# Overlapping feature tiles, B turned on its way from DRAM, and one packed state unit for two chunks, in a fused S5 scan and gated MLP

## The chip, the cores and the metric

The kernel runs on one core of a Trainium2 chip. The time is device time in microseconds from start to end of one execution; a lower number is better. In the profile PE is the matmul engine (PEld its weight loads), DVE the vector engine, ACT the scalar engine, POOL the general engine, and SP the engine that here only issues DMAs. Every engine works through its own list of instructions in order.

## The reference

Tokens x (2048 rows of 448 features, bf16) are normalised per row. The normalised rows xn go two ways, and the results are joined:

```python
xn = _layernorm(x)
# A: diagonal complex recurrence with 448 states
Bu = einsum("bld,pd->blp", xn + 0j, ((Lam_bar - 1.0) / Lam)[:, None] * Bmat)
h_t = Lam_bar * h_(t-1) + Bu_t
s = 2.0 * einsum("blp,dp->bld", hseq, Cmat).real + xn * Dskip
# B: gated MLP with 1792 inner features
h = sigmoid(xn @ w_gate) * (xn @ w_up)
g = silu(h @ w_down)
out = x + s * g
```

## The kernel before

The 2048 tokens are worked in four chunks of 512, which this document numbers 0 to 3 as the code does. A product over features needs features on partitions, so each chunk's xn is turned into `xnT[c]`, four tiles of 128 rows by 512 tokens (chunk 3 uses the buffer of chunk 0). Since 448 is three and a half times 128, the fourth tile holds the last 64 features twice, once in each half of the partitions: the columns 384 to 447 of xn are copied behind column 447 (`ln_turn`, `ln_twice`) before the turn. Chunk 0 is turned on PE, the other chunks by DMA turns on SP (L270).

**Work in half rows.** From the fifth feature group on, every product contracts 64 partitions at a time. PE runs a matmul on partitions 0-63 beside one on partitions 64-127 (`beside_each`); such a pair is called a slot here. A `Unit` is a list of products for the top half and one for the bottom half. `gu_unit(c, ft)` makes gate and up projection of one group of 128 inner features: 7 products in each half, two PSUM banks. `bu_unit(c, pt)` makes the inputs of the states: pt 0 to 2 hold 128 states each, real and imaginary part in a bank each, 7 and 7 products. The last 64 states (pt 3) hold real and imaginary part in the two halves of one bank, with 4 products on top and 3 below. `duo` runs two units: first the top of a beside the bottom of b, then the top of b beside the bottom of a. Both halves of a sum go to the same bank; when a sum changes halves, `Sum.add` sends a word over POOL so that the first half has ended.

**Order.** `emit_line` writes the order by hand. A positive number is a group of inner features, a negative one a state unit (-4 is pt 3). Chunks 1 to 3 run

```python
(0, -1), (1, -2), emit_downs, (2, 3), (4, -3), (5, 6), (-4, 7), (8, 9), (10, 11), (12, 13)
```

with `emit_downs` the down projection of the chunk before, and `emit_ys` the output product of the chunk before, behind (12,13) in chunk 1 and ahead of it in chunks 2 and 3. The eight PSUM banks are handed out in turn (`bank`). After a duo ACT empties its banks (`empty`: sigmoid or copy), and DVE multiplies (L737). The scan and its rotations (`bu_after`) are cut into pieces with a cost each; `fill` gives them out in the room that PE's slots leave, first come first served. `at` and `rest` hang other steps on a group: the normalisation of the next chunk, the turns, the mixing of C.

**B and C.** B is loaded into `raw["b_re"]` and `raw["b_im"]`, the last 64 columns are doubled, and SP turns it into `bT` by eight DMA turns (`emit_b`, L297), a pair per pt. C comes later into two raw buffers: c_re in the place called `raw_c`, c_im in `raw_re` (the place of b_re). It is turned behind groups 0 and 1 of chunk 1 (`emit_c_turn`, L169) and mixed with the state scales by `emit_c`: ACT writes a scaled copy (L482) into a temporary tile, DVE adds the other part (L483). The first three mixings hang on the second quarter of chunk 1's `emit_downs`. `c_room` gives the temporaries: the first two lie in `raw_im`, the place of b_im, the next two and the last in a pool, the fifth and sixth in `raw_c`.

**SP's order around this.** First x, weights for groups 0-3, B, weights for 4-7, x of chunk 1. Then the first two turns of B around the last weights (`load_w`, four DMAs a call: gate, up, and the last 64 rows of each, L122 and L126), the skip vector, the other turns, x of chunk 2, the turns of chunk 1's xn in two pairs with the last turns of B between them, `wd` (L1025), C (L165), and the swap of halves for unit -4 (L530).

Of the kernel before, what the change touches and what calls it, by code (L numbers as in the profile page):

```python
# [29 lines left out]
NPK = 2 * D  # L30
EPS = 1e-5
# [7 lines left out]
def swap_pair(ap: bass.AP) -> bass.AP:  # L39
    step_p, n_p = ap.ap[0]  # L40
    step_m, n_m = ap.ap[1]
    step_f, n_f = ap.ap[2]
    assert n_m == 2
    return bass.AP(tensor=ap.tensor, offset=ap.offset + step_m,
                   ap=[[step_p, n_p], [-step_m, n_m], [step_f, n_f]])

# [17 lines left out]
def kernel(  # L64
# [51 lines left out]
    def load_rows(eng, t, mat, f0, f1):  # L116
        eng.dma_start(out=t[:, 0:3, f0:f1], in_=mat[0:384, f0:f1].rearrange("(kt p) f -> p kt f", p=P))
        eng.dma_start(out=t[0:64, 3, f0:f1], in_=mat[384:448, f0:f1])

    def load_w(eng, f0, f1, between=None):  # L120
        for t, mat in ((wg, B_w_gate), (wu, B_w_up)):
            eng.dma_start(out=t[:, :, f0:f1], in_=mat[0:384, f0:f1].rearrange("(kt p) f -> p kt f", p=P))  # L122
        if between:
            between()
        for mat, p0 in ((B_w_gate, 0), (B_w_up, 64)):
            eng.dma_start(out=wt[p0:p0 + 64, f0:f1], in_=mat[384:448, f0:f1])  # L126
# [23 lines left out]
    for nm, mat in (("b_re", A_B_re), ("b_im", A_B_im)):  # L150
        raw[nm] = w.tile([P, KT, DP], BF16, name=nm, tag="raw" + nm[1:])
        load_rows(sync, raw[nm], mat, 0, D)
    dve.memset(raw["b_re"][:, :, D:DP], 0.0)
# [103 lines left out]
    def ln_norm(c, j):  # L257
        t = c * TPC + j
        xb = xn[c % 3]
        if c < 2:  # L260
            dve.tensor_scalar(out=xb[:, j, 0:D], in0=x_t[c][:, j, :], scalar1=mv[:, t, 0:1],
                              scalar2=rsd[:, t, :], op0=ALU.subtract, op1=ALU.mult)
        else:
            act.activation(xb[:, j, 0:D], x_t[c][:, j, :], ACT.Identity, bias=nmr[:, t, :],
                           scale=rsd[:, t, :])

    def ln_turn(c, j):
        xb, cols = xn[c % 3], slice(j * P, (j + 1) * P)
        if c > 0:
            sync.dma_start_transpose(out=xnT[c][:, 0:KT, cols], in_=xb[:, j, :])  # L270
            return
        (dve if j < 2 else pool).tensor_copy(out=xb[:, j, D:DP], in_=xb[:, j, 384:D])
        for kt in range(KT):
            pe.transpose(tps[j % 2][:, kt, :], xb[:, j, kt * P:(kt + 1) * P], ident[:])  # L274

    def ln_twice(c, copy, j0=0, j1=TPC):
        copy(out=xn[c % 3][:, j0:j1, D:DP], in_=xn[c % 3][:, j0:j1, 384:D])
        for j in range(j0, j1):
            ln_turn(c, j)
# [6 lines left out]
    def emit_b_twice():  # L286
        t = raw["b_im"]
        act.copy(out=t[:, 0:3, D:DP], in_=t[:, 0:3, 384:D])
        act.copy(out=t[0:64, 3, D:DP], in_=t[0:64, 3, 384:D])

    def emit_b(cc, pt):
        n = P if pt < 3 else 64
        if cc == 0:
            p0 = pt * P
        else:
            p0 = D if pt == 3 else 512 + pt * P
        sync.dma_start_transpose(out=bT[:, :, p0:p0 + n], in_=raw[("b_re", "b_im")[cc]][0:n, pt, :])  # L297
# [109 lines left out]
    def emit_skip(c):  # L407

        t = xn[c % 3][:, :, 0:D]
        dve.tensor_tensor(out=t, in0=t, in1=bcast_mid(skip[:], TPC), op=ALU.mult)  # L410
# [46 lines left out]
    def emit_c(i):  # L457
# [9 lines left out]
        if not c_room:  # L467
            for nm in ("raw_im", "raw_c"):
                both = []
                c_room.extend((nm, both, k) for k in range(2))  # L470
                if nm == "raw_im":
                    c_room.extend((None, None, None) for _ in range(2))
            c_room.append((None, None, None))
# [55 lines left out]
    def swap_halves(o, i):  # L529
        sync.dma_start(out=o[0:64, :], in_=i[64:128, :])  # L530
        sync.dma_start(out=o[64:128, :], in_=i[0:64, :])

    def bu_unit(c, pt):
        u = Unit()
        psts = [bank("bu") for _ in range(2 if pt < 3 else 1)]
        sums = [Sum(t, 7) for t in psts]

        def ops(h, cc, n):
            lo, hi = bu_cols(pt, cc)
            return [(sums[cc], (bT[HALF[h], kt, lo:hi], xnT[c][HALF[h], kt, :], 0, TC))  # L540
                    for kt in range(n)]

        if pt < 3:
            u.top = ops(0, 0, 4) + ops(0, 1, 3)
            u.bot = ops(1, 0, 3) + ops(1, 1, 4)
        else:
            u.top, u.bot = ops(0, 0, 4), ops(1, 0, 3)
        u.empty, u.then = bu_after(c, pt, psts)
        return u

    def bu_after(c, pt, pst):
# [5 lines left out]

        def then():
            unread[0] += 1
            assert unread[0] <= 4  # L560
            stream[0] += 1
            popped[stream[0]] = clock[0]
            pieces.extend((*p, stream[0]) for p in line)
# [62 lines left out]
        else:  # L626
            bus = sp.tile([P, TC], BF16, name="bus3", tag="bus", bufs=4)
            bsw = sp.tile([P, TC], BF16, name="bsw3", bufs=1)

            def empty_3():  # L630
                act.copy(out=bus[:], in_=pst[0][:])
                swap_halves(bsw, bus)

            empty = [empty_3]

            def q0():
                T["ta"] = sp.tile([P, TC], BF16, name="ta3", tag="ta")
                dve.tensor_tensor(out=T["ta"][:], in0=bus[:], in1=cosT[:, 3, :], op=mul)

            def q1():  # L640
                T["tb"] = sp.tile([P, TC], BF16, name="tb3", tag="tb")
                dve.tensor_tensor(out=T["tb"][:], in0=bsw[:], in1=spm[:, 3, 0, :], op=mul)
                unread[0] -= 1
# [26 lines left out]
            def q7():  # L670
                h = ht.tile([P, TC], BF16, name="h3")
# [3 lines left out]
            for cost, f, wait in ((0.42, q0, 1), (0.42, q1, 2), (0.42, q2, 0), (1.27, q3, 0), (0.42, q4, 0),  # L675
                                  (0.42, q5, 3), (0.34, q6, 0), (0.42, q7, 0)):
                later(cost, f, wait)
        return empty, then
# [13 lines left out]
    def gu_halves(c, ft, gt, ut, first, n0=0, n1=TC):  # L692
        f0, f1 = ft * P, (ft + 1) * P
        for t, p0 in ((gt, 0), (ut, 64)):
            pe.matmul(t[:, n0:n1], lhsT=wt[p0:p0 + 64, f0:f1],  # L695
                      rhs=xnT[c][p0:p0 + 64, 3, n0:n1], start=first, stop=not first)

    def gu_wholes(c, ft, gt, ut, first, n0=0, n1=TC, which=(0, 1)):
        f0, f1 = ft * P, (ft + 1) * P
        for t, wm in [((gt, wg), (ut, wu))[i] for i in which]:  # L700
            for kt in range(3):
                pe.matmul(t[:, n0:n1], lhsT=wm[:, kt, f0:f1], rhs=xnT[c][:, kt, n0:n1],  # L702
                          start=(first and kt == 0), stop=(not first and kt == 2))
# [14 lines left out]
    def gu_unit(c, ft):  # L718
# [6 lines left out]
        def ops(h, i, tail):  # L725
            x = xnT[c]
            o = [(sums[i], ((wg, wu)[i][HALF[h], kt, f], x[HALF[h], kt, :], 0, TC)) for kt in range(3)]
            return o + [(sums[i], (wt[HALF[h], f], x[HALF[h], 3, :], 0, TC))] * tail
# [61 lines left out]
    def y_ops(c, j, rows, d0=0, d1=D, skipped=False):  # L790
        sl = slice(j * P, (j + 1) * P)
        o = [(ident[rows, :], xn[c % 3][rows, j, d0:d1], d0, d1)] if skipped else []
# [21 lines left out]
    def emit_two(c, j):  # L814

        xb, two = xn[c % 3][:, j:TPC:2, 0:D], slice(j, TPC, 2)
        o = op_.tile([P, 2, D], BF16, name="o_t")
        for i in range(2):
            dve.tensor_tensor(out=o[:, i, :], in0=ys[c, j + 2 * i][:], in1=xb[:, i, :], op=ALU.add)  # L819
# [8 lines left out]
    def emit_rest_of(c, j):  # L828
        t = op_.tile([P, D], BF16, name="t_g", tag="zb", bufs=4)
        dve.tensor_tensor(out=t[:], in0=xn[c % 3][:, j, 0:D], in1=gs[c][:, j, :], op=ALU.mult)  # L830
        if j % 2 == 0:
            room_of_rests.append(w.tile([P, 2, D], FP32, name="t_x", tag=("raw_re", "raw_im")[j // 2]))
# [62 lines left out]
    def ln_plan(c):  # L895
# [16 lines left out]
        at(own, "down0", 0.0, lambda: ln_twice(c, act.copy))  # L912
# [62 lines left out]
    for pt in (0, 1, 3):  # L975
# [4 lines left out]
        if pt == 0:  # L980
            emit_b_twice()
# [25 lines left out]
    emit_b(0, 0)  # L1007
    load_w(sync, 1024, F, lambda: emit_b(1, 0))
    sync.dma_start(out=skip[:], in_=A_Dskip.partition_broadcast(P))
    for pt in range(1, KT - 1):  # L1010
        for cc in range(2):
            emit_b(cc, pt)
# [3 lines left out]
    def second_chunk(j0):  # L1016
# [3 lines left out]
        ln_twice(1, dve.tensor_copy, j0, j0 + 2)  # L1020

    at(0, 7, 1.0, lambda: second_chunk(0))
    at(0, 7, 0.0, lambda: [emit_b(cc, KT - 1) for cc in range(2)])
# [26 lines left out]
    def duo(c, a, b):  # L1050


        top, bot = a.top + b.top, b.bot + a.bot
        n = len(a.top)
        for u, t0, t1 in ((a, 0, n), (b, n, len(top))):
            beside_each(top[t0:t1], bot[t0:t1])
            if u is b:
                for i in range(2):
                    for v in (a, b):
                        if i < len(v.empty):  # L1060
                            v.empty[i]()
# [6 lines left out]
            if u is b:  # L1068
                a.then()
                b.then()  # L1070


    def emit_line(c, line):
        for p in line:
            if callable(p):
                p(c - 1)
            else:
                duo(c, *[bu_unit(c, -1 - k) if k < 0 else gu_unit(c, k) for k in p])

    emit_line(0, ((4, 5), (6, 7), (-1, 8), (-2, 9), (-3, 10), (11, 12), (-4, 13)))  # L1080
    for c in range(1, NCH):
        ends = ((12, 13), emit_ys) if c == 1 else (emit_ys, (12, 13))
        emit_line(c, ((0, -1), (1, -2), emit_downs, (2, 3), (4, -3), (5, 6), (-4, 7), (8, 9), (10, 11), *ends))
# [66 lines left out]
```

## Time and profile before

| what | value |
|---|---|
| median of three runs | 184.19 us (184.07 to 184.24) |
| span of the profiled execution | 182.6 us, granted clock 1.000 |
| the profiled execution's own time | not given beside its span; the median lies 1.6 us above the span |
| PE busy | 177.7 us, 1644 matmuls |
| DVE busy | 165.0 us |
| ACT busy | 114.1 us |
| POOL busy | 24.5 us |
| bytes moved by DMA | 15.07 MB |

A line of the timeline gives start, duration, engine, line of the kernel, operation, output and input, shape and count, and in brackets how long the engine stood before it and for whom. A line of the waits names who waited for whom, the sum in us, how many times, and the longest. A matmul's duration runs to the modelled end of its way through the array, so the distance between starts, and not the duration, tells the pace of PE. SP's lines are the times in which it issues a transfer, not the transfer itself.

### The profile page before, as it was taken

How to read it: one execution, taken by the hardware profiler on the slowest of the kernel's cores; microseconds unless marked ns; L12 is line 12 of the kernel's file. 1: busy time of each engine (PE TensorE's matmuls, PEld its weight loads, DVE VectorE, ACT ScalarE, POOL GpSimd, SP SyncE). 2: the span in 40 equal slices, each digit the busy share in tenths (PEclk: the TensorE clock that was granted, in tenths of full speed). 3: DMA queues.
4: the chain of work that ended last, by engine and by line, in shares of the span. 5: the costliest groups of instructions: out<-in, count | busy, mean ns of one | idle time of the engine just before them, and what ended most of it. 6: DMA issues, size and time to landing. Idle time of an engine off the chain costs nothing.

```text
span 182.6 us, 4348 instructions
## 1 busy us (share of the span) xinstructions
PE 177.7 (97%) x1644; PEld 98.3 (54%) x1644; DVE 165.0 (90%) x337; ACT 114.1 (63%) x236; POOL 24.5 (13%) x61
## 2 busy tenths in 40 slices
PE   7999999999999999999999999999999999999992
PEld 7776644446654444645654445545665544645552
DVE  4899999799989979999999999599999999699983
ACT  3999577979487787997367766057048567144100
POOL 4768546321000000004000000000000000000000
PEclk9999999999999999999999999999999999999999
DMA  5999997895434113011251010030001000011112
GB/s 152 312 307 252 231 161 106 229 311 111 104 76 89 29 32 101 4 52 52 41 79 29 4 29 0 4 101 0 4 2 29 4 13 17 4 50 50 29 36 68
DMA packets 27659, 15.07 MB, mean 83 GB/s; under 512 B 16243, under 2 KB 27638, under 8 KB 27638
## 3 DMA queue, kind: packets, MB, share of 16 engines
q1 hardware_dynamic: 27632, 14.79, 35.1%
q8 instruction: 13, 0.21, 0.5%
q14 instruction: 8, 0.07, 0.2%
q10 hardware_dynamic: 6, 0.00, 0.0%
HBM read 8.49 MB, written 1.84 MB: 57 GB/s over the span
## 4 chain that ended last, share of the span: by engine, by line
PE 97%; DVE 1%; POOL 0%; issue 0%; POOLq 0%; DVEq 0%
PE g_ps L510 25%; PE u_ps L510 19%; PE d_ps L510 17%; PE bu L510 12%; PE y_ps L510 11%; PE d_ps L1093 6%; PE warm_ps L192 2%; PE g_ps L702 2%; PE u_ps L702 1%; PE tp_x L274 1%; PE g_ps L695 1%; DVE sg L846 0%; DVE o_l L852 0%; DVE xnT L282 0%; POOL ident L129 0%
## 5 line engine op out<-in xcount | busy, mean ns | idle before, releaser
L510 PE MATMUL u_ps<-xnT,wu 64*128 64x512 bf16 x312 | 68.9, 376 | 0.0
L510 PE MATMUL g_ps<-xnT,wg 64*128 64x512 bf16 x312 | 62.0, 376 | 0.0
L740 ACT ACTIVATE sig<-g_ps 128x512 bf16<-128x512 f32 x52 | 29.1, 597 | 29.1 <-PE g_ps L510 29.1
L510 PE MATMUL bu<-xnT,bT 64*128 64x512 bf16 x196 | 45.7, 376 | 0.0
L510 PEld LDWEIGHTS <-wu 64*128 64x128 bf16 x312 | 25.3, 94 | 17.8 <-POOLq L512 1.6
L510 PE MATMUL d_ps<-wd,hF 64*128 64x448 bf16 x336 | 32.9, 349 | 0.0
L510 PEld LDWEIGHTS <-wg 64*128 64x128 bf16 x312 | 22.7, 94 | 17.6 <-POOLq L512 1.9
L740 ACT CAST ub<-u_ps 128x512 bf16<-128x512 f32 x52 | 29.3, 604 | 0.8 <-DVE hF L712 0.8
L510 PEld LDWEIGHTS <-hF 64*128 64x128 bf16 x336 | 19.9, 94 | 12.1
L510 PEld LDWEIGHTS <-bT 64*128 64x128 bf16 x196 | 17.7, 94 | 10.7
L510 PE MATMUL y_ps<-ct,h 64*128 64x448 bf16 (+2 forms) x203 | 22.7, 343 | 0.0
L589 DVE TENSOR_TENSOR_SCAN wv<-r_col,st,ta 128x512 bf16<-128x512 f32 x18 | 22.6, 1274 | 0.1
L737 DVE TENSOR_TENSOR hF<-sig,ub 128x512 bf16<-128x512 bf16 x52 | 20.9, 416 | 1.3 <-ACT ub L740 1.1
L510 PE MATMUL u_ps<-xnT,wt 64*128 64x512 bf16 x52 | 19.6, 376 | 0.0
L510 PE MATMUL g_ps<-xnT,wt 64*128 64x512 bf16 x52 | 19.6, 376 | 0.0
L510 PEld LDWEIGHTS <-h 64*128 64x128 bf16 (+1 forms) x203 | 13.4, 95 | 8.0
L570 ACT CAST bus<-bu 128x512 bf16<-128x512 f32 x24 | 14.3, 595 | 2.3 <-PE g_ps L510 2.3
L764 ACT ACTIVATE sigd<-d_ps 128x448 bf16<-128x448 f32 x12 | 6.6, 550 | 12.4 <-PE d_ps L510 12.4
L238 POOL TENSOR_TENSOR rsd<-ve,mhalf 128x1 f32<-128x1 f32 (+2 forms) x8 | 7.5, 932 | 48.5 <-PE u_ps L510 45.6
L510 PEld LDWEIGHTS <-wt 64*128 64x128 bf16 x104 | 9.8, 94 | 5.5 <-DMA wt<-in_B_w_up_dram 0.4
L1093 PE MATMUL d_ps<-wd,hF 128*128 128x448 bf16 x56 | 10.9, 353 | 0.0
L819 DVE TENSOR_TENSOR o_t<-y_ps,xn 128x448 bf16<-128x448 f32 x12 | 6.9, 618 | 3.7 <-PE y_ps L510 3.7
(153 smaller groups left out, 229.8 us busy)
## 6 DMA issues: line engine op xcount, KB each, us to landing
wd<-in_B_w_down_dram SPq DMA_DIRECT2D x1, 1568.0 KB, 7.6
x<-in_A_x_dram SPq DMA_DIRECT2D x3, 448.0 KB, 5.5
out_dram<-o_t SPq DMA_DIRECT2D x6, 224.0 KB, 2.1
wg<-in_B_w_gate_dram SPq DMA_DIRECT2D x2, 384.0 KB, 4.4
wu<-in_B_w_up_dram SPq DMA_DIRECT2D x2, 384.0 KB, 5.3
wg<-in_B_w_gate_dram SPq DMA_DIRECT2D x1, 576.0 KB
wu<-in_B_w_up_dram SPq DMA_DIRECT2D x1, 576.0 KB, 8.6
bsw<-bus SPq DMA_DIRECT2D x8, 64.0 KB, 2.0
```

What stands on the lines that cost most here:

```text
L192: pe.matmul(warm_ps[:], lhsT=ident[:], rhs=ident[:], start=True, stop=True)
L238: pool.tensor_tensor(out=rsd[:, t:t + n, :], in0=ve[:, t:t + n, :], in1=mhalf[:, 0:n, :], op=ALU.pow)
L274: pe.transpose(tps[j % 2][:, kt, :], xb[:, j, kt * P:(kt + 1) * P], ident[:])
L510: m = pe.matmul(self.t[:, n0:n1], lhsT=lhsT, rhs=rhs, start=self.done == 1, stop=self.done == self.n)
L570: empty = [lambda cc=cc: act.copy(out=bus[:, cc, :], in_=pst[cc][:]) for cc in range(2)]
L589: dve.tensor_tensor_scan(out=T["wv"][:, cc, :], data0=rb, data1=T["ta"][:, cc, :], initial=(0.0 if c == 0 else st[pt][:, cc, :]), op0=mul, ...
L702: pe.matmul(t[:, n0:n1], lhsT=wm[:, kt, f0:f1], rhs=xnT[c][:, kt, n0:n1], start=(first and kt == 0), stop=(not first and kt == 2))
L737: dve.tensor_tensor(out=h[:], in0=sig[:], in1=ub[:], op=ALU.mult)
L740: u.empty = [lambda: act.activation(sig[:], gt[:], ACT.Sigmoid), lambda: act.copy(out=ub[:], in_=ut[:])]
L764: act.activation(sigd[:], ds[j][:], ACT.Sigmoid)
L819: dve.tensor_tensor(out=o[:, i, :], in0=ys[c, j + 2 * i][:], in1=xb[:, i, :], op=ALU.add)
L1093: pe.matmul(ds[j][:], lhsT=hF[c, ft][:, j * P:(j + 1) * P], rhs=wd[:, ft, :], start=ft == 0, stop=ft == FT - 1)
```

## The change

- **Feature tiles.** The four tiles of xnT now start at features 0, 128, 192 and 320, so the middle two overlap: features 192 to 255 lie in the bottom of tile 1 and the top of tile 2. Gate takes tiles 0, 2, 3 whole and the top of tile 1; up takes tiles 0, 1, 3 whole and the bottom of tile 2. For chunks 1 to 3 the normalisation writes 512 columns (0 to 255 and 192 to 447) in place of 448 and a copy; readers of xn step over the doubled columns.
- **B.** It is no longer loaded and doubled. Sixteen DMA turns of 256 columns read it from DRAM. The place `raw_im` is gone; c_im is the first to use `raw_re`, and the first two temporaries of the mixing lie in `raw_re`.
- **Weights.** `load_w` has six DMAs a call, the row ranges in the new order.
- **State unit -4.** It is made for chunks 0 and 1 at once in chunk 0, for 2 and 3 in chunk 2, with two banks and 7 and 7 products, one exchange of halves for both and one list of pieces.
- **Order.** `duo` becomes `group`, and chunks 1 and 3 run (5, 6, 7) as a group of three.

```diff
+K_ROWS = (0, 128, 192, 320)
+GATE_K, UP_K = (0, 2, 3), (0, 1, 3)
+def two_runs(ap: bass.AP, step: int, n: int) -> bass.AP:
+    return bass.AP(tensor=ap.tensor, offset=ap.offset, ap=[*ap.ap[:-1], [step, 2], [1, n]])
...
+        eng.dma_start(out=wg[:, 1:3, f0:f1], in_=rows(B_w_gate, 192, 448))
+        eng.dma_start(out=wg[:, 0, f0:f1], in_=rows(B_w_gate, 0, 128))
+        eng.dma_start(out=wu[:, 0:2, f0:f1], in_=rows(B_w_up, 0, 256))
+        eng.dma_start(out=wu[:, 2, f0:f1], in_=rows(B_w_up, 320, 448))
+        eng.dma_start(out=wt[0:64, f0:f1], in_=rows(B_w_gate, 128, 192))
+        eng.dma_start(out=wt[64:128, f0:f1], in_=rows(B_w_up, 256, 320))
...
-    for nm, mat in (("b_re", A_B_re), ("b_im", A_B_im)):
-        raw[nm] = w.tile([P, KT, DP], BF16, name=nm, tag="raw" + nm[1:])
-        load_rows(sync, raw[nm], mat, 0, D)
-    dve.memset(raw["b_re"][:, :, D:DP], 0.0)
...
     def ln_norm(c, j):
+            xb, src = two_runs(xb, 2 * P, 2 * P), two_runs(src, 192, 2 * P)
...
-        (dve if j < 2 else pool).tensor_copy(out=xb[:, j, D:DP], in_=xb[:, j, 384:D])
...
-    def ln_twice(c, copy, j0=0, j1=TPC):
-        copy(out=xn[c % 3][:, j0:j1, D:DP], in_=xn[c % 3][:, j0:j1, 384:D])
...
-    def emit_b_twice():
...
-        sync.dma_start_transpose(out=bT[:, :, p0:p0 + n], in_=raw[("b_re", "b_im")[cc]][0:n, pt, :])
+            for kt in (0, 2):
+                sync.dma_start_transpose(out=bT[:, kt:kt + 2, p0:p0 + n],
+                                         in_=mat[pt * P:pt * P + n, K_ROWS[kt]:K_ROWS[kt] + 2 * P])
...
-            for nm in ("raw_im", "raw_c"):
+            for nm in ("raw_re", "raw_c"):
...
     def bu_unit(c, pt):
+        psts = [bank("bu") for _ in range(2)]
+            x = xnT[c + i * (pt == 3)]
...
+    def bu_pair_after(c, psts):
+        bus = sp.tile([P, 2, TC], BF16, name="bus3", tag="bus", bufs=4)
+        bsw = sp.tile([P, 2, TC], BF16, name="bsw3", bufs=1)
+        a, b = [bu_after(c + i, 3, (bus[:, i, :], bsw[:, i, :])) for i in range(2)]
+        def empty(i):
+            act.copy(out=bus[:, i, :], in_=psts[i][:])
+            if i == 1:
+                swap_halves(bsw, bus)
...
+                h = ht.tile([P, TC], BF16, name="h3", bufs=3)
...
-    def duo(c, a, b):
+    def group(c, units):
+        top = sum((u.top for u in units), [])
+        bot = sum((u.bot for u in units[1:] + units[:1]), [])
+        t0, last = 0, len(units) - 1
+        for k, u in enumerate(units):
+            t1 = t0 + len(u.top)
             beside_each(top[t0:t1], bot[t0:t1])
+            whole = [units[0]] * (k == last) + [u] * (k > 0)
+            for i in range(2):
+                for v in whole:
+                    v.empty[i]()
...
+        mid = ((5, 6), (-4, 7)) if c == 2 else ((5, 6, 7),)
+        emit_line(c, ((0, -1), (1, -2), emit_downs, (2, 3), (4, -3), *mid, (8, 9), (10, 11), *ends))
```

## The prediction

> **What bounds the kernel now.** I read the page's busy shares first, then the chain, then the waits of each engine, then the timeline of SP, ACT and PE around the places that the change touches.
>
> ```profile
> PE 177.7 (97%) x1644; PEld 98.3 (54%) x1644; DVE 165.0 (90%) x337; ACT 114.1 (63%) x236; POOL 24.5 (13%) x61
> ...
> PE 97%; DVE 1%; POOL 0%; issue 0%; POOLq 0%; DVEq 0%
> ```
>
> TensorE is busy 97% of the span and the chain that ends last runs through it almost alone. So a change gains only what it takes off PE, and loses whatever makes PE stand. PE's list of waits holds 1.3 us at the very start and this one line:
>
> ```profile
> PE g_ps L702 <- DVE xnT L282: 0.2, 1, 0.2
> ```
>
> PE works in slots: a matmul on rows 0-63 beside one on rows 64-127. With 512 columns, starts lie 0.2157 us apart (group (4,-3): 14 slots from 54.61 to 57.63). The exception is the group with unit -4:
>
> ```profile
> 61.52 0.38 PE L510 MATMUL bu<-xnT,bT 64*128 64x512 bf16 x1
> 61.79 0.39 PE L510 MATMUL g_ps<-xnT,wg 64*128 64x512 bf16 x1
> ...
> 62.45 0.38 PE L510 MATMUL bu<-xnT,bT 64*128 64x512 bf16 x1
> 62.73 0.39 PE L510 MATMUL u_ps<-xnT,wu 64*128 64x512 bf16 x1
> ```
>
> Two of its steps are 0.27 and 0.28 instead of 0.2157 (the sum whose other half just ended), some 0.06 each; chunk 0 shows the same at 33.30 and 34.23.
>
> On ACT the mixing of C (L482) stands until the turned c_re has landed, and the emptying of the down banks is queued behind it:
>
> ```profile
> 48.22 1.23 ACT L482 ACTIVATE c_tmps<-tc_re,nci 128x448 f32<-128x448 bf16 x2 [2.58 <-DMA tc_re<-c_re]
> 49.35 0.65 ACT L482 ACTIVATE c_tmp<-tc_re,nci 128x448 f32<-128x448 bf16 x1
> 49.91 0.52 ACT L764 ACTIVATE sigd<-d_ps 128x448 bf16<-128x448 f32 x1
> ...
> 53.30 0.55 ACT L766 CAST zb<-d_ps 128x448 bf16<-128x448 f32 x1
> ```
>
> From the end of that wait to the end of the last emptying it is 5.63 us, of which 0.29 waited for PE: 5.34 of work. DVE gives the moment at which the turned c_im landed, 54.1:
>
> ```profile
> 54.19 1.28 DVE L483 SCALAR_TENSOR_TENSOR ct<-tc_im,ncr,c_tmps 128x448 bf16<-128x448 bf16 x2 [0.84 <-DMA tc_im<-c_im]
> ```
>
> SP issues without a break from 0.7 to 39 us, so what is added there moves all that follows:
>
> ```profile
> 9.86 1.29 SPq L297 DMA_TRANSPOSE bT<-b_re  x1
> ...
> 29.08 2.53 SPq L270 DMA_TRANSPOSE xnT<-xn  x2
> 31.66 0.57 SPq L1025 DMA_DIRECT2D wd<-in_B_w_down_dram  x1
> ```
>
> **The change part by part.** *Start (PE).* xn of chunk 0 needs no doubled columns: two DVE copies (198 ns each) and two POOL copies (236 ns each) go. The first pair lies on the way to the wait at L702, the second on the way to the last turned tile at 9.16. The same time is gained twice, not added: about -0.3. Ends: 0 (if the weights' first tiles, now issued in more pieces, become the wait) and -0.5.
>
> *Packing.* Four groups of 11 slots and three of 14, 86 slots, become 14+21+28+21 = 84: -0.43. The eight long steps go too, since in the new units a sum's two halves lie at least four slots apart: 8 x 0.06 = -0.5. Together -0.9; ends -0.43 and -0.93.
>
> *Banks after a group of three.* It takes six of the eight banks, so the group behind it, (8,9), gets back the banks of unit 5, which finished only at its end. In the trace's duo (5,6) the third emptying on ACT ends 0.9 us after the group (61.78 against 60.87). The fourth slot of (8,9) wants that bank at +0.65: a stand of some 0.3 in chunk 3. In chunk 1 a mixing (0.7, L482) is queued between and pushes it to about 0.85. Together +1.1. Ends 0 (if banks are handed out otherwise) and +1.2.
>
> *Work per token.* The normalisation writes 512 columns for 448 (ACT 775 ns, DVE 391 ns each; by share of columns 0.11 and 0.06 more); the copies L277 go (ACT 2 x 0.40, DVE 2 x 0.19), b's copies too (0.6 on ACT). All of this lies beside PE. The skip and sum operations keep their element counts. Unit -4's DVE work (4 us a chunk) moves from chunks 1 and 3 into 0 and 2; the planner feeds it from a queue, h3 has a third buffer, and the readers are a chunk later: nothing. Its cover is the chunk between writer and reader; DVE's queue would have to lag by tens of us to matter. POOL carries the same number of half-to-half words (28 sums of bu before and after), and SP's swaps of bus become four larger for eight, where it idles.
>
> *SP.* Three weight loads have six DMAs for four, at the pitches of their rows (0.57, 0.60, 0.68 us a DMA): +3.7. The four loads of B go: 4.41 to 6.76, -2.35 (and 0.78 MB off engines that the windows show 100% and more busy from 4.6 to 27 us). Eight turns of B, which with gaps hold SP 12.6 us in all, become 16 of half the columns from DRAM, at t each. The skip load, x and the turns of xn keep their places. The issue of wd then comes at 31.66 + 3.7 - 2.35 - 12.6 + 16t = 20.4 + 16t. No row shows a turn from DRAM. Bounds: a plain issue, 0.40, below; a whole turn, 1.24, above, as 64 rows cost no less than 128 (the two turns of the last 64 rows took 1.79 and 1.19). I take 0.62, half of a turn's undisturbed 1.24, because the rows show no dependence on rows, so columns remain, and the slow ones came with full DMA engines: wd at 30.3.
>
> [...]
>
> *The wait added.* c_tmps of the first two mixings moves from raw_im (long free) to raw_re, which now holds raw c_im. ACT can write there only when all four turns of c_im have landed, not those of c_re: 54.1 by the trace instead of 48.2. Queued behind it on ACT: the third mixing and the eight emptyings of the down banks, 5.34 us. PE waits for those: group (4,-3) starts at 54.61 and needs the last down bank three slots on, at 55.26. PE itself comes +0.07 (start and one long step -0.45, three more slots in chunk 0 less its own long steps +0.52). So ACT must be released by 55.33 - 5.34 = 50.0. SP's lead of 1.3 us brings c_im's landing to 52.8: PE stands 2.8 us. Ends: 0, and 4.1 if SP has no lead. The lead can't go below about 51.9, as the turns of C also stand behind the swap at L530, which waits for ACT until some 37.3 and ends near 38.9. DVE stands at the gates (L769) for the same time, in step with PE, so it costs nothing further; nothing gives PE the time back.
>
> *Chunk 1's xnT.* The packed unit reads it at slot 4 of (-4,13), about 32.9, where before 34.5 was enough. Before, its last turn is issued at 30.35 and lands 2.8 later, 33.15; with SP's lead 31.8. It costs 0 up to t = 0.69.
>
> Sum: -0.3 - 0.9 + 1.1 + 2.8 = +2.7 on a span of 182.6, 185.3. The medians' 184.19 lies 1.6 above the profiled span, which I add: **186.9 us**.
>
> **The rivals.** *The wait for c_im is hidden (faster).* If the landing comes before 50.0, or the wait covers only a part of the old tile, 2.8 goes; if the bank wait also fails, 184.2 - 1.2 = 183.0. For it: DMA engines are freed of 0.78 MB in the crowded stretch. Against: the eight turns of C alone hold SP from 41.16 to 52.90 and can't start before about 38.9; only faster turns than these rows, or a wait for the first two turns alone, bring it below 51.9. It decides at 50.0. Chance 0.2. With the bank wait left it is 184.1, no change: 0.1.
>
> *Turns from DRAM cost nearly as much as whole ones.* At t = 0.84 (a plain 0.45 and half of the rest) wd comes at 33.8, xnT of chunk 1 lands 2.4 late, and the c_im wait is 3.9: 190.4. At 1.24 it is 8.8 and 3.9: 196.8. For it: 64 rows cost what 128 do. Against: the columns, which are halved, are all that is left to set the time. It decides at 0.69. Chance 0.18. [...]
>
> *The packing saves nothing,* because DVE becomes the bound in chunk 2 with 4 us more: DVE stands 3.7 us in L819 over the run, enough cover for most; worth at most +1, folded into the forecast.
>
> **How the numbers follow.** The forecast (c_im wait of 1.5 to 4) has 0.52 and its own range 185.5 to 188.3; dear turns 0.18 (188.3 to 196.8); hidden 0.2 (182.8 to 183.8); balanced 0.1 (183.8 to 184.8). A difference of 0.2%, 0.4 us, is about what can be told from none. Leaving out a tenth at each end gives 183.2 to 190.0. Faster 0.2; same 0.08 (the balanced case less its upper edge); slower 0.72.
>
> **What would show it.** ACT's wait before L482 should name tc_im and end near 52.8, with a gap of 2 to 3 us in PE at the start of (4,-3); no such gap, and the main term is wrong. SP's turns of bT should last near 0.6. The groups of three should be followed by gaps of some 0.3 and 0.85 in PE, and no long steps be left in the group of unit -4. PE's first g_ps should start near 6.5. A gap in bu near 33 would show the dear turns.

## The result and the profile after

The changed kernel takes **197.59 us** (median of four runs, 196.89 to 199.34) against 184.22 us (184.07 to 184.53) before: a ratio of **1.073, 95% interval 1.068 to 1.078**. Slower, as forecast, but 10.7 us beyond the forecast of 186.9 and outside its range. The profiled execution took 197.9 us with a span of 196.1, against 182.6 before; so the profile shows 13.5 us to be found.

The page of the changed kernel: busy times, granted clock in 40 slices, and the chain that ended last.

```profile
PE 181.7 (93%) x1644; PEld 100.5 (51%) x1644; DVE 164.4 (84%) x332; ACT 113.5 (58%) x232; POOL 23.0 (12%) x59
...
PEclk9999999966999999999999999999999999999999
...
PE 62%; SPq 20%; DMA 7%; ACT 5%; DVE 2%; issue 2%; ACTq 0%; DVEq 0%
```

Before, the chain was 97% PE. Now a fifth of it is SP issuing transfers, and PE's share of busy time fell although its busy microseconds rose by 4. The two sixes in the clock row (39 to 49 us) give a part of that rise: there PE ran at a lower clock, and its matmuls lasted longer (0.63 at 44.17 against 0.38 at 36.91). The first product of chunk 0's `emit_ys` starts 14.1 us later than before (86.30 against 72.24), the first of the last down projection 13.4 us later (176.37 against 163.00). So all of the loss lies before chunk 0's output, in chunk 0 and at the group (4,-3) of chunk 1.

SP's timeline (start, time of issue, how many) shows where it begins:

```profile
9.27 2.56 SPq L294 DMA_TRANSPOSE bT<-in_A_B_re_dram  x2
11.87 3.92 SPq L294 DMA_TRANSPOSE bT<-in_A_B_im_dram  x2
...
33.80 2.51 SPq L294 DMA_TRANSPOSE bT<-in_A_B_re_dram  x2
36.34 2.51 SPq L294 DMA_TRANSPOSE bT<-in_A_B_im_dram  x2
38.95 2.52 SPq L279 DMA_TRANSPOSE xnT<-xn  x2
41.52 0.57 SPq L1034 DMA_DIRECT2D wd<-in_B_w_down_dram  x1
```

A turn of half the columns holds SP for 1.24 us (the median of the sixteen), as long as a whole one before (1.19 to 1.29 in five of the eight, more in the other three); the four turns of 64 rows of B, from 33.80 to 38.85, are no cheaper. `wd`, the mark that I forecast at 30.3 and that stood at 31.66 before, is issued at 41.5. What hangs on these turns waits. PE's list of waits (us in all, times, longest):

```profile
PE bu L509 <- DMA bT<-in_A_B_im_dram: 2.6, 3, 1.4
PE bu L509 <- DMA xnT<-xn: 2.0, 1, 2.0
PE bu L509 <- ACT sig L749: 1.9, 2, 1.6
...
PE g_ps L509 <- ACT zb L775: 0.9, 1, 0.9
```

The first three did not exist before. The wait put down to `sig`, at 38.90, is also one for bT: it ends 2.59 us after the issue of the last two turns of B's real part (36.31). In the run with moved temporaries, below, these are issued until 36.75 and the same matmul starts at 39.35, again 2.60 later, while that `sig` runs only after it, from 39.56 on. PE's timeline around them, and at (4,-3):

```profile
32.37 0.39 PE L509 MATMUL bu<-xnT,bT 64*128 64x512 bf16 x1 [1.35 <-DMA bT<-in_A_B_im_dram]
...
38.90 0.37 PE L509 MATMUL bu<-xnT,bT 64*128 64x512 bf16 x1 [1.61 <-ACT sig L749]
...
40.15 0.38 PE L509 MATMUL bu<-xnT,bT 64*128 64x512 bf16 x1 [0.64 <-DMA bT<-in_A_B_im_dram]
...
42.94 0.58 PE L509 MATMUL bu<-xnT,bT 64*128 64x512 bf16 x1 [1.95 <-DMA xnT<-xn]
...
43.31 0.63 PE L509 MATMUL bu<-xnT,bT 64*128 64x512 bf16 x1
...
43.74 0.63 PE L509 MATMUL bu<-xnT,bT 64*128 64x512 bf16 x1
...
67.95 0.37 PE L509 MATMUL g_ps<-xnT,wg 64*128 64x512 bf16 x1 [0.92 <-ACT zb L775]
68.81 0.37 PE L509 MATMUL bu<-xnT,bT 64*128 64x512 bf16 x1 [0.49 <-ACT zb L775]
...
70.55 0.37 PE L509 MATMUL u_ps<-xnT,wu 64*128 64x512 bf16 x1 [0.50 <-ACT zb L775]
```

Read two things here beside the brackets. From 42.94 on, starts lie 0.43 us apart instead of 0.2157, until 47.16. The windows show the same as a clock, a mean over each stretch (columns: length, PE, PEld, DVE, ACT and POOL busy with counts, granted clock, DMA share, GB/s):

```profile
35.00:44.00 9.00, 4.80 (x36) 1.64 (x34) 5.84 (x15) 5.28 (x15) 0.78 (x4) 0.80 0.34 64
44.00:55.00 11.00, 11.00 (x92) 5.37 (x90) 5.37 (x10) 6.63 (x13) 2.19 (x6) 0.85 0.99 248
```

And a stand costs more than its bracket even at full clock: a matmul takes 0.38 from start to modelled end, and the next would have started 0.2157 after it, so each stand adds 0.16.

Chunk 0's half-row groups start at 14.05 and would take 98 slots, 21.1 us, to 35.2; they end near 47.2, 12.0 late. Stands in L509: 0.16 + 0.35 + 0.29 + 0.48 + 0.56 + 1.35 + 1.61 + 0.64 + 1.95 = 7.4. Eight of them at full clock add 8 x 0.16 = 1.3, and two short ones without a bracket 0.3. The half clock adds 10 x 0.21 = 2.1, and 0.4 at its onset. That is 11.5 of the 12.0. The stand at (4,-3) is 1.9 and 3 x 0.16.

That one is the wait which the prediction named. ACT's timeline:

```profile
65.27 1.23 ACT L481 ACTIVATE c_tmps<-tc_re,nci 128x448 f32<-128x448 bf16 x2 [7.83 <-DMA tc_im<-c_im]
...
69.92 0.58 ACT L775 CAST zb<-d_ps 128x448 bf16<-128x448 f32 x1
```

ACT stands for the turned c_im, and the emptyings of the down banks, queued behind, release PE.

### The profile page after: what moved, and what is told of

Same layout as the page of the kernel before. It is cut to its first block, busy times and chain, and to the rows that moved or that the text cites. A ratio compares the mean times of both kernels' runs of the same rounds, so it can differ in the third digit from the quotient of the medians.

```text
span 196.1 us, 4349 instructions
## 1 busy us (share of the span) xinstructions
PE 181.7 (93%) x1644; PEld 100.5 (51%) x1644; DVE 164.4 (84%) x332; ACT 113.5 (58%) x232; POOL 23.0 (12%) x59
## 4 chain that ended last, share of the span: by engine, by line
PE 62%; SPq 20%; DMA 7%; ACT 5%; DVE 2%; issue 2%; ACTq 0%; DVEq 0%
PE g_ps L509 16%; PE u_ps L509 13%; PE d_ps L509 11%; PE y_ps L509 11%; SPq L294 8%; PE bu L509 6%; PE d_ps L1104 5%; SPq L172 5%; DMA c_re<-in_A_C_im_dram 5%; DMA bT<-in_A_B_im_dram 2%; DMA tc_im<-c_im 1%; ACT zb L775 1%; SPq L133 1%; SPq L128 1%; ACT sig L749 1%
## 5 line engine op out<-in xcount | busy, mean ns | idle before, releaser
L509 PE MATMUL u_ps<-xnT,wu 64*128 64x512 bf16 x312 | 62.4, 381 | 0.7 <-ACT zb L775 0.5
L509 PE MATMUL g_ps<-xnT,wg 64*128 64x512 bf16 x312 | 55.5, 379 | 0.9 <-ACT zb L775 0.9
L509 PE MATMUL bu<-xnT,bT 64*128 64x512 bf16 x196 | 47.6, 390 | 7.4 <-DMA bT<-in_A_B_im_dram 2.6
L509 PEld LDWEIGHTS <-wu 64*128 64x128 bf16 x312 | 23.9, 95 | 17.4 <-DMA wu<-in_B_w_up_dram 1.1
L509 PE MATMUL d_ps<-wd,hF 64*128 64x448 bf16 x336 | 32.3, 349 | 0.0
L509 PEld LDWEIGHTS <-wg 64*128 64x128 bf16 x312 | 21.0, 95 | 16.8 <-issue 2.2
L509 PEld LDWEIGHTS <-bT 64*128 64x128 bf16 x196 | 18.1, 97 | 21.5 <-issue 8.1
L509 PEld LDWEIGHTS <-hF 64*128 64x128 bf16 x336 | 18.8, 94 | 13.1
L509 PE MATMUL y_ps<-ct,h 64*128 64x448 bf16 (+2 forms) x203 | 22.2, 343 | 0.0
L509 PE MATMUL u_ps<-xnT,wt 64*128 64x512 bf16 x52 | 19.8, 382 | 0.4 <-DMA wt<-in_B_w_up_dram 0.4
L509 PE MATMUL g_ps<-xnT,wt 64*128 64x512 bf16 x52 | 19.8, 381 | 0.0
L509 PEld LDWEIGHTS <-h 64*128 64x128 bf16 (+1 forms) x203 | 12.9, 95 | 8.5
L241 POOL TENSOR_TENSOR rsd<-ve,mhalf 128x1 f32<-128x1 f32 (+2 forms) x8 | 7.0, 874 | 52.5 <-PE bu L509 49.6
L509 PEld LDWEIGHTS <-wt 64*128 64x128 bf16 x104 | 9.9, 95 | 5.8 <-DMA wt<-in_B_w_up_dram 0.7
```

What stands on the lines that cost most here:

```text
L241: pool.tensor_tensor(out=rsd[:, t:t + n, :], in0=ve[:, t:t + n, :], in1=mhalf[:, 0:n, :], op=ALU.pow)
L509: m = pe.matmul(self.t[:, n0:n1], lhsT=lhsT, rhs=rhs, start=self.done == 1, stop=self.done == self.n)
```

## The experiments

The first question was what makes a turn cost 1.24 us: the turn itself, or that it reads from DRAM. The second was how the 13.4 us are shared among turns, the wait for c_im, and the rest. The runs were made in three sets, in which the kernel before took 184.22, 184.39 and 184.65 us; of a difference between runs of two sets, up to 0.4 us can be the set's.

### Half-width turns in the kernel before

```diff
-        sync.dma_start_transpose(out=bT[:, :, p0:p0 + n], in_=raw[("b_re", "b_im")[cc]][0:n, pt, :])
+        for kt in (0, 2):
+            sync.dma_start_transpose(out=bT[:, kt:kt + 2, p0:p0 + n],
+                                     in_=raw[("b_re", "b_im")[cc]][0:n, pt, kt * P:(kt + 2) * P])
```

> The kernel before with each of its eight turns of B, still read from the on-chip copy, cut into two of 256 columns; nothing else. Theory 1, a turn holds SP some 1.24 us whatever its columns and wherever it reads: SP issues wd near 41.8 instead of 31.7, chunk 1's turned xn lands some 10 late against a need at 34.5, so PE stands about 9 us and the half clock after that adds 1 to 2: 194 to 196 us. Theory 2, it is the reading from DRAM that makes a turn of half the columns cost what a whole one did: turns here take near 0.62 and the time stays at 184.2. In both the wait of the mixing is on c_re and costs nothing.

Measured: 192.89 us (191.70 to 194.11), ratio 1.046 (1.040 to 1.053), 1.1 us below what the first theory had. SP's timeline of the execution at 191.70:

```profile
27.06 2.54 SPq L298 DMA_TRANSPOSE bT<-b_im  x2
...
32.88 2.51 SPq L298 DMA_TRANSPOSE bT<-b_re  x2
35.44 2.52 SPq L298 DMA_TRANSPOSE bT<-b_im  x2
...
40.62 0.57 SPq L1027 DMA_DIRECT2D wd<-in_B_w_down_dram  x1
```

Source in SBUF, half the columns, and again a median of 1.24 a turn. Eight more turns delay `wd` by 9.0 us, 1.1 each. So DRAM is not what makes them dear, and the split alone costs 8.5 us in a kernel where nothing else changed.

### The changed kernel with B loaded and turned whole

B comes by eight plain loads into tiles that already have the overlapping layout, and eight turns from SBUF follow.

```diff
-            for kt in (0, 2):
-                sync.dma_start_transpose(out=bT[:, kt:kt + 2, p0:p0 + n],
-                                         in_=mat[pt * P:pt * P + n, K_ROWS[kt]:K_ROWS[kt] + 2 * P])
+            sync.dma_start_transpose(out=bT[:, :, p0:p0 + n], in_=raw[("b_re", "b_im")[cc]][0:n, pt, :])
```

> The changed kernel with B loaded to the chip in the overlapping layout by eight plain loads and turned from there by eight turns of 512 columns; b_im lies where c_re comes later, all else as changed. Theory 1 (a fixed price per turn): SP loses 8 x 1.27 and gains 8 x 0.55, wd at about 35.9; chunk 1's turned xn lands near 37.4 against 33, a stand of some 4.5 with the clock; c_im's wait of 2 to 4 stays: 189 to 192. Theory 2 (reading from DRAM is dear) gives the same within 1 us. If neither, and the six-piece weight loads are the cause, it stays near 197.6.

Measured: 193.18 us (192.88 to 194.10), ratio 1.048 (1.045 to 1.052). The issues of SP, and PE's first stand:

```profile
24.87 1.26 SPq L301 DMA_TRANSPOSE bT<-b_re  x1
26.18 1.27 SPq L301 DMA_TRANSPOSE bT<-b_im  x1
...
36.79 0.57 SPq L1040 DMA_DIRECT2D wd<-in_B_w_down_dram  x1
```

```profile
15.53 0.82 PE L515 MATMUL g_ps<-xnT,wg 64*128 64x512 bf16 x6 [1.40 <-DMA wg<-in_B_w_gate_dram]
```

The stands for bT are gone, with a turn of 512 columns (1.22 to 1.30) at the same price as one of 256. But eight loads ahead of the weights bring a new wait (1.40, and 0.77 for wt), the last turn of xnT is still late (0.86), and the stand at (4,-3) grows to 2.5 + 0.5 + 0.5. The new waits put the time above the 189 to 192 that was expected. The run still gains 4.4 us on the changed kernel, and it shows that DMAs taken out of SP's list at one place should not be added at an earlier one.

### Six tall turns from DRAM

The same bytes from the same place, in turns of up to 448 rows by 256 columns.

```diff
+        rows = {0: ((0, 0, 448, 0), (1, 0, 384, 512)), 3: ((1, 384, 448, 448),)}.get(pt, ())
+        for cc, r0, r1, p0 in rows:
+            for kt in (0, 2):
+                sync.dma_start_transpose(out=bT[:, kt:kt + 2, p0:p0 + r1 - r0],
+                                         in_=(A_B_re, A_B_im)[cc][r0:r1, K_ROWS[kt]:K_ROWS[kt] + 2 * P])
```

> The changed kernel with B turned from DRAM by six turns of up to 448 rows by 256 columns in place of sixteen of up to 128 rows. Theory 1 (a fixed price per turn): SP loses 10 x 1.27, wd is issued near 29, no stand is left in chunk 0, c_im's wait leaves 1 to 3 us: 184.5 to 186.5. If the price goes by what is turned, in rows or in bytes, SP gains nothing and it stays at 195 to 198.

Measured: 189.20 us (187.71 to 190.42), ratio 1.028 (1.021 to 1.035). The rows by line give shortest, median and longest issue in ns:

```profile
L293 SPq DMA_TRANSPOSE bT<-in_A_B_im_dram x4: 1226/1622/2053, 14.0 to 26.4; - x4
L293 SPq DMA_TRANSPOSE bT<-in_A_B_re_dram x2: 1326/2242/3157, 9.4 to 10.8; - x2
```

The first, 448 rows, took 1.33, one of 384 rows 1.28; the shortest, 1.23, has 64. With three and a half times the rows of an ordinary turn the issue starts from nearly the same floor. The longest, 3.16, is the second of 448 rows, issued at 10.81; in the changed kernel a turn of 128 rows took 2.62 at 11.87, with a DMA share of 1.04 from 9 to 14 us. But in all the six hold SP for 11.0 us, 1.8 each, the sixteen for 21.7, 1.4 each: whether the tall ones are dearer by their size or by where they stand was not separated. Six turns instead of sixteen return 8.4 us, `wd` goes out at 31.16, and no stand for bT or xnT is left. The time lies above the 184.5 to 186.5 that was expected. Even the fastest execution, the one profiled (187.71, full clock), has stands of 1.26, 0.31 and 0.24 at the weights, which now go out behind four dear turns, and two of 0.49 at (4,-3); two others, with mean clocks of 0.990, took 190.3 and 190.4.

### The temporaries of the mixing moved

```diff
-            for nm in ("raw_re", "raw_c"):
+            for nm in ("raw_c", "raw_re"):
                 both = []
                 c_room.extend((nm, both, k) for k in range(2))
-                if nm == "raw_re":
+                if nm == "raw_c":
                     c_room.extend((None, None, None) for _ in range(2))
```

The first two temporaries now lie over c_re, which the first mixing needs turned in any case.

> The changed kernel with the two places of the mixing's temporaries exchanged: the first two lie where raw c_re was, the fifth and sixth where raw c_im was. The theory that the stand at group (4,-3) comes from ACT waiting for the turns of c_im: ACT waits for c_re alone, some 5.8 us shorter, PE has no gap at (4,-3), 195.4 to 195.9. The rival, that these gaps come from the backlog of the stands in chunk 0, leaves 197.6.

Measured: 194.87 us (194.22 to 196.06), ratio 1.058 (1.053 to 1.062): 2.7 us back, half a us more than was expected. ACT's wait for c_im and the stand at (4,-3) are gone, the stands of chunk 0 stay (1.18 for wu, 0.54, 0.68, 1.30 and 0.64 for bT, 2.20 for xnT).

The same wait was also put into the kernel before, where nothing else is late:

```diff
-            for nm in ("raw_im", "raw_c"):
+            for nm in ("raw_re", "raw_c"):
                 both = []
                 c_room.extend((nm, both, k) for k in range(2))
-                if nm == "raw_im":
+                if nm == "raw_re":
```

> The kernel before with the first two temporaries of the mixing in the place of raw c_im, and nothing else. By the prediction's step ACT may write there at 54.1 instead of 48.2, against a latest 49.9, and PE stands 4.2 us at (4,-3): 188.2 to 188.6. If PE catches the delay up elsewhere, or the wait covers only the first turns, 184.2 to 186.

Measured: 189.32 us (189.00 to 191.43), ratio 1.027 (1.023 to 1.032), 4.7 us. The execution profiled is the longest of the four, 191.43, 6.8 above the kernel before. ACT, then PE, then the windows (PE is the second number, the clock the third from the end):

```profile
55.30 1.23 ACT L482 ACTIVATE c_tmps<-tc_re,nci 128x448 f32<-128x448 bf16 x2 [9.39 <-DMA tc_im<-c_im]
```

```profile
57.98 0.58 PE L510 MATMUL g_ps<-xnT,wg 64*128 64x512 bf16 x1 [2.72 <-ACT zb L766]
58.85 0.58 PE L510 MATMUL bu<-xnT,bT 64*128 64x512 bf16 x1 [0.28 <-ACT zb L766]
```

```profile
56.00:60.00 4.00, 1.74 (x7) 0.57 (x8) 1.56 (x4) 4.00 (x10) 0.00 (x0) 0.74 0.48 98
60.00:64.00 4.00, 4.00 (x21) 1.37 (x19) 3.93 (x9) 3.12 (x8) 0.00 (x0) 0.50 0.00 0
```

The stand itself is 3.0, less than the 4.1 of the prediction's upper bound, although c_im here let ACT go at 55.3 and not at 54.1. PE came back at half clock and so asked for the last bank later: its first up product starts at 60.58, just after the last emptying ends at 60.52, without a stand. The slots take 0.43 until 64.4, some 15 of them; that is 3.2 us and the other part of this execution's price. The mean clock was 0.982 here and 0.991 in the other three, which took 189.0 to 189.6. From these clocks, (1 - 0.991) x 187 us gives 1.7 us lost to the clock in each of them, against 3.4 here; that is an estimate, as no trace of them is kept.

### Tall turns and moved temporaries together

> The changed kernel with both suspects taken away: six tall turns of B and the temporaries exchanged. If they carry the loss, the stand at (4,-3) goes (1.5 us in the run with tall turns) and what is left is the late last weights at 21.8 (1.8 us): 185 to 187.5. If a third cause is at work, it stays near 188 to 189.

Measured: 186.09 us (185.56 to 186.77), ratio 1.008 (1.005 to 1.011). With both edits 11.5 of the 13.4 us are back. What is left stands at the weights of groups 4 to 7:

```profile
21.31 0.39 PE L508 MATMUL g_ps<-xnT,wg 64*128 64x512 bf16 x1 [0.68 <-DMA wg<-in_B_w_gate_dram]
22.35 0.39 PE L508 MATMUL u_ps<-xnT,wu 64*128 64x512 bf16 x1 [0.22 <-DMA wu<-in_B_w_up_dram]
23.77 0.39 PE L508 MATMUL u_ps<-xnT,wt 64*128 64x512 bf16 x1 [0.35 <-DMA wt<-in_B_w_up_dram]
```

Those weights are six DMAs instead of four, behind four dear turns.

### The packed unit and the groups of three alone

The kernel before keeps its feature tiles, weight loads and SBUF turns; it gets `group`, the packed unit -4 and the new order. b_im goes to `raw_c`, so that the first two temporaries have a free place, and one more small ACT copy doubles the last columns of b_re.

```diff
-    def duo(c, a, b):
+    def group(c, units):
...
-        emit_line(c, ((0, -1), (1, -2), emit_downs, (2, 3), (4, -3), (5, 6), (-4, 7), (8, 9), (10, 11), *ends))
+        mid = ((5, 6), (-4, 7)) if c == 2 else ((5, 6, 7),)
+        emit_line(c, ((0, -1), (1, -2), emit_downs, (2, 3), (4, -3), *mid, (8, 9), (10, 11), *ends))
```

> The kernel before with the packed unit -4 and the groups of three alone: feature tiles, B and weights as before, one copy more for b_re's doubled columns on ACT; to make room b_im lies in the place of c_re, and the mixing's first two temporaries lie there too (its wait is on c_re as before). By my working PE saves 2 slots and eight long steps, 0.93 us, and chunk 1's turned xn comes just in time: 183.2 to 183.6. If the group behind a group of three has to wait for its banks, as the prediction had it, 184.2 to 184.6.

Measured: **183.42 us** (183.18 to 183.99) against 184.65 in the same set, ratio **0.993 (0.991 to 0.995)**, within what was expected without a bank wait. This part of the change makes the kernel faster, by 0.9 to 1.7 us, under one per cent but clear of the noise, and this version beats both kernels. Its page:

```profile
PE 176.8 (97%) x1644; PEld 95.6 (52%) x1644; DVE 164.5 (90%) x337; ACT 114.4 (63%) x237; POOL 24.2 (13%) x61
```

PE is 0.9 us less busy than before with as many matmuls, as the working of the packing had it: two slots and the long steps. DVE's share is what it was, so it does not take over as the bound.

## Why the prediction was right in its sign and wrong in its size

**Steps that held.** The kernel became slower. The wait for c_im exists, with the chain as told: ACT at L481 waits for tc_im, the down banks are emptied late, PE stands at (4,-3). I had 2.8 us for it, and taking it out returns 2.7, but that the two agree is luck: the 2.8 took SP to be 1.3 us ahead of the kernel before, and in the run SP was 9.9 behind and PE 12.0. In a kernel with no other delay it costs 4.7, above the 4.1 of my upper end; by the estimate given there, 1.7 of it is the half clock behind the stand, for which the prediction had no term. The packing was forecast at -0.9; alone it gives 0.9 to 1.7, and in the changed kernel the undisturbed pair of chunks shows its half: over chunk 2, with the longer unit, the lag behind the kernel before grows by 0.5, over chunk 3 it shrinks by 1.0. No long step is left in chunk 2's group of unit -4 (117.30 to 120.32), and the work moved on DVE and POOL shows in no new wait of PE. By the prediction's sum these steps together make a small loss; no run shows that sum alone.

**The step that failed** is the price of a turn on SP, t = 0.62, taken because "the rows show no dependence on rows, so columns remain". The inference skipped a third case: that neither sets the time. Rows of 64 and 128 with the same issue time were the hint, and it speaks for a fixed price as much as for columns. Measured, t has a median of 1.24 with 64 or 128 rows of 256 columns, from DRAM or from SBUF, and 1.25 with 512 columns in the run that turned B whole; 448 rows took 1.33 at the least. The formula of the prediction, 20.4 + 16t, gives 40.2 for `wd` at 1.24, and it came at 41.5. The two terms in it miss in opposite ways: the turns with their gaps hold SP for 22.5, 2.7 more than 16 x 1.24, and all else ahead of `wd` for 19.0 as before, where the working had 1.35 more (3.7 for the weights' pieces less 2.35 for B's loads). The rival of the dear turns at t = 1.24 gave 196.8; the run gave 197.59. So the mechanism stood in the text with too low a chance, 0.18, but the closeness of the number is in part luck, as the parts below show.

**How the loss was made up.** The rival counted 8.8 for xnT and 3.9 for c_im. In truth 12.0 lie in chunk 0 and 2.4 at (4,-3), less about 1.0 for the packing. It was not the last turn of xnT alone: PE stood at every pair of bT in turn, each time for what SP was short. And because chunk 0 lost so much, chunk 1 came later and its wait for c_im shrank. The rival also had 1.1 for a bank wait that did not come, and nothing for the half clock, which is 2.5 of the 12.0; so its sum came near by parts that are off in both directions.

**Terms that were not there.** The start gained 0.14 instead of 0.3: the first half-row group starts at 14.05, before at 14.19. The first g_ps, forecast near 6.5, starts at 6.86 (6.79 before). The bank wait after a group of three, +1.1, did not come at all, neither in the changed kernel nor in the packing alone; no stand of PE lies at (8,9). The trace of chunk 3 shows why:

```profile
162.22 1.08 ACT L749 CAST ub<-u_ps 128x512 bf16<-128x512 f32 x2
...
162.56 1.00 PE L509 MATMUL u_ps<-xnT,wu 64*128 64x512 bf16 x6
```

The up product of unit 9 starts at 162.56, while ACT still empties the up banks of units 5 and 7 (162.22 to 162.81 and 162.68 to 163.30). Handed out strictly in turn, the bank of unit 5 would be the one it needs; so the banks are not handed out like that. The prediction had named this as its lower end, 0. In the reckoning of when ACT must be released, "start and one long step -0.45" is 0.36 by its own terms; it changes nothing.

**What stays open.** The tall turns with moved temporaries still lie 2.7 us above the packing alone by medians; 1.4 by the profiled executions, of which the three stands at the weights are 1.25. Whether the overlapping feature tiles would pay with weights and turns ordered better was not tried. What makes one turn in several take 1.5 us and more was not found either.

## What to carry to other kernels

In the runs here a turn of B held SP for 1.17 us at the least, and one of 448 rows for 1.33: count the issues, not the bytes alone, and follow the one in-order list behind them down to the first product that waits. Where a row shows that one dimension does not set a cost, test whether any does, before the cost is given to the other dimension. A change made of several parts should be priced and run part by part; here a gain of 1.2 us lay under a loss of 14.

## What the runs showed of the hardware

- **A turn's issue has a floor that its size hardly moves.** Most turns of B hold SP for 1.17 to 1.33 us, for 64 to 448 rows, 256 or 512 columns, SBUF or DRAM. Some take more: 2.62 at 11.87 in the changed kernel, where the DMA share from 9 to 14 us is 1.04, but also 1.77 at 26.14 there, where the share from 26 to 28 us is 0.17; with six tall turns 3.16 at 10.81 and 2.05 at 26.44. The loads of weights in the changed kernel take 0.43 to 0.59.
- **A stand of PE costs more than its length.** In the changed kernel each adds 0.16 us at full clock, since a matmul of 512 columns lasts 0.38 and the next could have started after 0.2157. And the clock can halve: after a stand of 2.72 us in the kernel before with the added wait, slots took 0.43 until 64.4, over 6 us, with a granted clock of 0.50 from 60 to 64. In the changed kernel they turn slow at 40.36 (a matmul of 0.59, then up to 0.63), after stands of 1.61 and 0.64, and stay so through a further 1.95 until 47.16. In the changed kernel with B turned whole, slots are slow from 17.12 to 20.08 (matmuls of 0.60 to 0.63) after stands of 1.40 and 0.77. The half-width turns in the kernel before show 2.07 and 0.77 close together and full clock throughout in the execution profiled, while the other three of that kernel had mean clocks of 0.98 to 0.99. So no one length decides in these runs, and executions of one kernel differ.
